# Half-height second score products in an fp32r attention and FFN kernel, and another order of a tick's stages

## The chip, the cores and the metric

The kernel runs on one NeuronCore of a Trainium2 chip. The metric is the device time of one execution in microseconds. Before the change the median of three runs is 1044.72 us (1044.53 to 1045.08). A separate execution with the hardware profiler on supplies the rows that are read below.

## The reference

```python
scores = scale * np.matmul(q, k.transpose(0, 1, 3, 2))      # 8 batches, 8 heads, 576 x 64
mask = (rel >= 0) & (rel < 128)                             # causal, window of 128
attn = softmax(np.where(mask, scores + bias, -1e9))         # bias: ALiBi slopes per head
x = np.matmul(attn, v)                                      # -> (4608, 512)
h = x @ w_in                                                # 512 -> 2048
out = (h * sigmoid(1.702 * h)) @ w_out                      # 2048 -> 512
```

All inputs are float32. A row of queries sees at most 128 keys, so a block of 128 queries needs two blocks of 128 keys.

## The kernel before

TensorE's fast format here is fp32r, which keeps fewer bits than fp32. To keep the precision, an operand x is split into a high part (x cast to fp32r) and a low part (x minus that, again in fp32r), and a product is put together from several fp32r products.

**Blocks and units.** Batch 0 is treated apart, in plain fp32 (units that the code calls whole). For batches 1 to 7, two heads of 576 rows lie side by side as one head pair of 1152 rows, cut into nine blocks of 128 queries. A unit is one or two successive blocks: for batches 2 to 7 each pair has four units of two blocks and one unit of one block. A block's scores have 256 columns (its own keys and those before), the first block of a pair 128.

**The operands of a score product.** q and k come in transposed and doubled: the 64 features stand in partitions 0 to 63 and again in 64 to 127. `split_q` (L770) casts the whole doubled q to fp32r into the tile Q; `split_rest` (L792) casts k into K1, replaces the lower half of Q (partitions 64 to 127) by q's low part, and writes k minus K1 into K2, again doubled. So in Q one half holds the high part and the other half the low part, and a product over 128 partitions adds both at once. `scores` (L819) issues two products for each block, K1 and then K2, both with Q's 128 rows, accumulated in one PSUM bank that both blocks share (`s_ps`, one buffer):

```python
for z, ks in enumerate((u.K1, u.K2)):
    nc.tensor.matmul(to, u.Q.t[:, q], ks.t[:, k], start=(z == 0), stop=(z == 1))
```

The fourth of these partial products, low times low, comes along for free.

**The other stages of a unit.** `biased` (L860, DVE) adds bias and mask and takes the row minimum; `exponents` (L879, ACT); `normal` (L890, POOL, DVE or ACT) multiplies by the reciprocal of the sum; `flip` (L912, TensorE) transposes the probabilities into a PSUM buffer `t_ps`, of which there are two (tag "t"); `high` and `low` (L938, L943) split the transposed probabilities; `load_v` and `split_v` bring in and split the values; `mix` (L953) multiplies by them, and `sum_up` (L985) adds the halves and, for later rows, stores the result to DRAM by a DMA from SP's queue.

**What sets the order.** A software pipeline works on several units at once: `tick` (L1260) issues each stage for another unit, so that a unit passes through in about five ticks. Between ticks come the FFN's steps: `up` (L1068, 12 products for one 128-wide slice of the 2048) and `down` (L1184). The loop at L1331 runs through the FFN's steps and calls as many ticks as the due times ask. Each operation goes into a plan with an estimated duration. Up to 340 us of planned time (`CUT`) the planner's greedy `order` (L325) fixes the order of every engine's queue by these estimates; the rest is issued in the plan's own order (`rest`, L425) and placed by the framework's scheduler. PSUM has eight banks: two accumulators of the FFN, two for `h_ps`, one each for `s_ps` and `x_ps`, two for `t_ps`.

**Array forms.** A matmul's operands fix which part of the array of TensorE it uses. The profile writes it as rows*columns: 128*128 for most, 64*128 for operands of 64 partitions. In batch 0, where a head's 64 features are the contraction, score products (L850) are 64*128; some of its mix products (L967) are 128*64, or 64*128 for a last chunk of 64 keys.

Of the kernel before, what the change touches and what calls it, by code (L numbers as in the profile page):

```python
# [8 lines left out]
F32 = mybir.dt.float32  # L9
# [10 lines left out]
B, H, S, D = 8, 8, 576, 64  # L20
DM, DFF = 512, 2048
NT = B * S
P = 128
HALF = P // 2
NP = H // 2
# [25 lines left out]
LAX = {"w": 1000, "hi": 800, "lo": 0, "gl": 300, "cast": 0, "xl": 600, "p": 500}  # L51
# [7 lines left out]
SAFE = 60  # L59
REST = 400  # L60
FAR = 7
PACE = 32
LATE = 14
FAST = {c: range(0, 7) if c > LATE else range(2, 7) for c in range(LATE, NCH)}
# [400 lines left out]
def tile_kernel(ctx: ExitStack, tc: tile.TileContext, q0, k0, v0, qT, kT, v, w_in, w_out, out):  # L465
    nc = tc.nc
# [9 lines left out]
    add = plan.add  # L476

    def buf(pool, shape, dtype, tag, slots=1, name=None):
        return Buf(plan, pool, shape, dtype, tag, slots, name)
# [9 lines left out]
    def act_cast(n):  # L489
        return 104 + 0.8 * n  # L490
# [10 lines left out]
    def pool_two(n):  # L501
        return 140 + 2.17 * n

    def copy_on(e, dst, src):
        (nc.scalar.copy if e == "ACT" else nc.vector.tensor_copy)(dst, src)  # L505

    def less_on(e, dst, a, b):
        (nc.gpsimd if e == "POOL" else nc.vector).tensor_tensor(dst, a, b, ALU.subtract)  # L508
# [13 lines left out]
    def less_ways(n):  # L522
        return {"DVE": (dve_one(n), True)}
# [246 lines left out]
    def split_q(u):  # L770
        if u.whole:
            return
        u.Q = buf(att, [P, 2 * P], F32R, "Q", 2)
        add("ACT", lambda e: copy_on(e, u.Q.t[:, :u.nq], u.rq.t[:, :u.nq]), act_cast(u.nq), r=[u.rq], w=[u.Q],
            chain="split_q", ways=cast_ways(u.nq), behind=gates[32 * 2 - 1 - 32])

    def split_v(u):
# [10 lines left out]
        for i, c in enumerate(u.loaded):  # L788
            c.vbuf = u.VV
            c.v = lambda i=i, c=c: u.VV.t[:c.n, i].rearrange("p a d -> p (a d)")  # L790

    def split_rest(u):  # L792
        if u.whole:
            return
        u.K1 = buf(att, [P, 3 * P], F32R, "K1", 2)
        u.K2 = buf(att, [P, 3 * P], F32R, "K2", 2)
        add("ACT", lambda e: copy_on(e, u.K1.t[:, :u.nk], u.rk.t[:, :u.nk]), act_cast(u.nk),
            r=[u.rk], w=[u.K1], chain="K1", ways=cast_ways(u.nk), auto="DVE")
        add("POOL", lambda e: less_on(
            e, u.Q.t[D:, :u.nq], u.rq.t[D:, :u.nq], u.Q.t[D:, :u.nq].bitcast(F32)), pool_two(u.nq),  # L800
            r=[u.rq], w=[u.Q], port=True, chain="Q", ways=less_ways(u.nq), lax=LAX["lo"])
        add("POOL", lambda e: less_on(
            e, u.K2.t[:, :u.nk], u.rk.t[:, :u.nk], u.K1.t[:, :u.nk].bitcast(F32)), pool_two(u.nk),
            r=[u.rk, u.K1], w=[u.K2], port=True, chain="K2", ways=less_ways(u.nk), lax=LAX["lo"])
# [13 lines left out]

    def scores(u):  # L819
        if early(u):  # L820
            u.s = buf(ps, [P, 2, 2 * P], F32, "h", 2, name="s_h")
        else:
            u.s = buf(ps, [P, 2, 2 * P], F32, "s", 1, name="s_ps")
        ns = 0
        runs, reads = [], []
        for e, b in enumerate(u.blocks):
            n = b.end - b.first
            if u.whole:
                lo = b.q0 - u.at
                qr, q = columns(0, u, lo, b.rows)  # L830
                at, k = b.first, lo - P + b.first
                while at < b.end:
                    m = min(b.end - at, T - k % T)
                    kr, ks = columns(1, u, k, m)
                    runs.append((e, b, at, m, q, ks))
                    reads += [r for r in (qr, kr) if r not in reads]
                    ns += max(1.72 * m, 220)
                    at, k = at + m, k + m
            else:
                ko = b.q0 - P + b.first - u.k0  # L840
                qs = slice(b.q0 - u.q0, b.q0 - u.q0 + b.rows)
                ks = slice(ko, ko + n)
                ns += 2 * max(0.465 * n, 86)
                runs.append((e, b, b.first, n, qs, ks))

        def run():
            for e, b, at, n, q, k in runs:
                to = u.s.t[:b.rows, e, at:at + n]
                if u.whole:
                    nc.tensor.matmul(to, q(), k(), start=True, stop=True)  # L850
                else:
                    for z, ks in enumerate((u.K1, u.K2)):
                        nc.tensor.matmul(to, u.Q.t[:, q], ks.t[:, k], start=(z == 0), stop=(z == 1))  # L853

        u.scored = add("PE", run, ns, 165, r=reads if u.whole else [u.Q, u.K1, u.K2], w=[u.s],
            chain="scores", kind="S" if u.whole else "R")
        if early(u):
            u.scored.beside = units[u.n - 1].scored

    def biased(u):  # L860
        u.mins = small(u, 0, "mins")
        for e, b in enumerate(u.blocks):
            if first(u):
                b.p = Part(works[u.n // 2], (u.n % 2, e), lambda t, i=u.n % 2 * 2 + e: t[:, i])
            else:
                b.p = buf(att, [P, 2 * P], F32, "pb", 5)
            for head, ra, rb, cs in b.heads:
                if cs > b.live:
                    add("POOL", lambda b=b, ra=ra, rb=rb, cs=cs: nc.gpsimd.memset(b.p.t[ra:rb, b.live:cs], MOST),
                        230, w=[b.p.key_at()])  # L870
                on = ra if u.joined else 0
                add("DVE", lambda b=b, e=e, head=head, ra=ra, rb=rb, cs=cs, on=on: nc.vector.tensor_tensor_reduce(  # L872
                    b.p.t[ra:rb, cs:b.end], u.s.t[ra:rb, e, cs:b.end], bias[ra:rb, head, on + cs:on + b.end],
                    -SCALE, BIG, ALU.add, ALU.min, u.mins.t[ra:rb, e:e + 1]),
                    75 + 1.05 * (b.end - cs), 150, r=[u.s], w=[b.p.key_at(), u.mins.key_at(e)], chain="biased")
            if b.live > b.first:
                add("POOL", lambda b=b: nc.gpsimd.memset(b.p.t[:, :b.live], 0.0), 120, w=[b.p.key_at("z")])

# [376 lines left out]
            due.append((len(units), b * S // T, start) if b < 4 else (len(units), PACE * (b - 3), 5))  # L1255
    units += [None] * 4
    loads = [u for u in units if u and not u.whole]
    ticks = 0

    def tick():  # L1260

        nonlocal ticks
        n = ticks

        def stage(k, *steps):
            u = units[n + k] if 0 <= n + k < len(units) else None
            for step in steps:
                if u:
                    step(u)

        stage(1, split_q)
        stage(-2, flip, split_v)
        stage(0, load_v)
        stage(-1, biased)
        stage(1, split_rest)
        stage(-1, exponents)
        stage(-1, normal)
        stage(-2, high)
        stage(-2, low)
        stage(0, scores)  # L1280
        stage(-3, mix)
        if n + 1 < len(units) and units[n + 1] and not units[n + 1].whole and loads:
            load(loads.pop(0))
        ticks += 1
# [46 lines left out]
    for now, (j, f) in enumerate(flat):  # L1331

        if halves < 2 * NF:
            owed += max(
                (2 * g + 2 - halves - owed) / max(need[g] - DECODE_AHEAD - now, 1)
                for g in range(halves // 2, NF))
            while owed >= 1 and halves < 2 * NF:
                owed -= 1
                g, ws = halves // 2, (w1, w2)[halves % 2]
                fetch_upto(g + 1 + FETCH_AHEAD)  # L1340
                ws[g] = decode(ws[g], f"w{1 + halves % 2}_{g}", gates[2 * GATE - 1])
                halves += 1

        pace, last = 0.0, 0
        for n, by, start in due:
            if start > seen:
                break
            last = n + 3
            end = starts[by] if start != 5 else starts[6] + by
            pace = max(pace, (n + 3 - ticks - credit) / max(end - 1 - SLACK - now, 1))  # L1350
        credit += pace
        while credit >= 1 and ticks < last:
            credit -= 1
            tick()
        if j.c in FOLDS:
            if f == 2:
                folding = fold(FOLDS[j.c])
            if f > 1:
                next(folding, None)
        if f == 6 and FAR <= j.c + 1 < NCH:  # L1360
            fetch_x(j.c + 1)
        if j.c == LATE and f % 2 == 0 and f // 2 < 7:
            unfold((f // 2 + 2) % 7)
        if now + 1 < len(flat):
            nj, nf = flat[now + 1]
            if nj is j:
                j.up(nf)
            else:
                begin(nj)
                seen = max(seen, nj.c)  # L1370
        j.down(f)
        if f == j.f1 - 1:
            j.finish()

# [80 lines left out]
```

## Time and profile before

| | |
|---|---|
| median of three runs | 1044.72 us |
| the profiled execution | 1044.83 us, its span 1043.0 us |
| granted TensorE clock | 0.999 |
| TensorE busy | 1029.4 us, 99% of the span |
| weight loads | 937.7 us |
| DVE, ACT, POOL busy | 793.5, 655.8, 530.6 us |
| score products of batches 1 to 7 (L853) | 504 |
| they start between | 82.4 and 841.9 us |

Rows of a timeline give the start, the duration, engine, line, operation, the tile written and those read, the form of the array, the shape of the moving operand, and how many successive instructions were put together. Successive matmuls overlap, so a duration is the way of one through the array, while the interval from start to start is what it takes of TensorE's time. PEld is the load of the stationary operand, which can run under the matmul before it. Lines are those of the kernel before.

### The profile page before, as it was taken

What the parts mean: (1) busy time and instruction counts of PE and PEld (TensorE: products, weight loads), DVE (VectorE), ACT (ScalarE), POOL (GpSimd) and SP (SyncE); (2) the same over time, 40 slices, a digit from 0 to 9 for tenths busy, and PEclk for the clock granted to TensorE, in tenths of its full rate; (3) what the DMA queues carried; (4) which work ended last, traced back from release to release, by engine and by line L of the source; (5) the groups of instructions that cost most, each with busy time, mean ns of one, the idle gap of its engine ahead of it and who ended that gap; (6) DMA issues with size and microseconds to landing.
All of it is one profiled execution on the core that took longest, in us unless ns stands there. A gap on an engine that the chain in (4) does not pass through costs nothing.

```text
span 1043.0 us, 23177 instructions
## 1 busy us (share of the span) xinstructions
PE 1029.4 (99%) x7220; PEld 937.7 (90%) x7220; DVE 793.5 (76%) x2464; ACT 655.8 (63%) x1962; POOL 530.6 (51%) x804
## 2 busy tenths in 40 slices
PE   9999999999999999999999999999999999999998
PEld 5777888988888999999999999999999999999997
DVE  8999988899978888768686777768766744667574
ACT  7999877677745666666666666666666643344443
POOL 3343445344423467576666757666666623333342
PEclk9999999999999999999999999999999999999999
DMA  9734233333322333434333433424242354001000
GB/s 355 303 96 141 61 88 95 80 81 98 83 76 65 103 101 94 141 90 129 95 114 106 122 104 101 126 76 150 79 117 67 113 169 140 21 22 41 2 22 21
DMA packets 122027, 106.65 MB, mean 102 GB/s; under 512 B 48880, under 2 KB 111984, under 8 KB 121904
## 3 DMA queue, kind: packets, MB, share of 16 engines
q1 hardware_dynamic: 116720, 95.73, 31.2%
q10 hardware_dynamic: 5184, 9.44, 2.5%
q8 instruction: 57, 0.93, 0.4%
q14 instruction: 66, 0.54, 0.2%
HBM read 82.58 MB, written 22.54 MB: 101 GB/s over the span
## 4 chain that ended last, share of the span: by engine, by line
PE 88%; DVE 8%; issue 2%; ACT 2%; POOL 0%; DMA 0%; DVEq 0%; ACTq 0%; POOLq 0%
PE h_ps L1074 35%; PE acc L1197 28%; PE s_ps L853 5%; PE t_ps L928 5%; PE x_ps L973 5%; PE m L1162 3%; PE acc L1162 2%; PE s_ps L850 1%; PE x_ps L967 1%; DVE g L1091 1%; DVE wc L592 1%; DVE pb L872 1%; DVE w_ps L589 1%; PE idle L556 1%; DVE gl L508 1%
## 5 line engine op out<-in xcount | busy, mean ns | idle before, releaser
L1074 PE MATMUL h_ps<-xh,w 128*128 128x256 f32 x2304 | 358.7, 283 | 0.3
L1074 PEld LDWEIGHTS h_ps<-xh,w 128*128 128x128 f32 x2304 | 316.9, 188 | 18.4 <-DVE g L1091 1.7
L1197 PE MATMUL acc<-w,gh 128*128 128x512 f32 x928 | 259.5, 396 | 0.0
L1074 PE MATMUL h_ps<-xl,w 128*128 128x256 f32 x1152 | 187.3, 280 | 0.0
L508 POOL TENSOR_TENSOR gl<-g,gh 128x256 fp32r<-128x256 f32 x169 | 131.7, 781 | 107.5 <-ACT gh L505 68.2
L1197 PEld LDWEIGHTS acc<-w,gh 128*128 128x128 f32 x928 | 157.6, 189 | 19.3 <-issue 0.2
L1074 PEld LDWEIGHTS h_ps<-xl,w 128*128 128x128 f32 x1152 | 158.2, 188 | 2.3
L884 ACT ACTIVATE pb<-pb,mins 128x256 f32<-128x256 f32 (+2 forms) x272 | 132.3, 487 | 39.5 <-DVE mins L872 29.8
L508 POOL TENSOR_TENSOR Q<-rq,Q 64x256 fp32r<-64x256 f32 (+1 forms) x136 | 94.9, 698 | 117.9 <-issue 25.6
L1091 DVE SCALAR_TENSOR_TENSOR g<-g,h_ps 128x256 f32<-128x256 f32 x236 | 97.6, 413 | 72.5 <-ACT g L1090 70.9
L1090 ACT ACTIVATE g<-h_ps 128x256 f32<-128x256 f32 x236 | 90.1, 382 | 92.7 <-PE h_ps L1074 69.7
L1197 PE MATMUL acc<-w,gl 128*128 128x512 f32 x464 | 148.1, 397 | 0.0
L508 POOL TENSOR_TENSOR K<-rk,K 128x384 fp32r<-128x384 f32 (+1 forms) x121 | 109.7, 907 | 69.8 <-ACT Q L505 23.8
L505 ACT CAST gh<-g 128x256 fp32r<-128x256 f32 x184 | 74.6, 405 | 66.8 <-DVE g L1091 60.5
L872 DVE CUSTOM_DVE_ANT_0 pb<-s_ps,bias 128x256 f32<-128x256 f32 (+2 forms) x304 | 110.6, 377 | 5.5 <-PE s_ps L853 1.6
L853 PE MATMUL s_ps<-K,Q 128*128 128x256 f32 (+1 forms) x504 | 92.0, 298 | 2.4 <-DVE mins L872 1.4
L928 PE MATMUL t_ps<-ident,pb 128*128 128x128 f32 x516 | 91.0, 273 | 2.7 <-DVE wc L592 2.4
L505 ACT CAST ph<-t_ps 128x512 fp32r<-128x512 f32 (+2 forms) x133 | 68.8, 518 | 34.3 <-PE t_ps L928 25.7
L1197 PEld LDWEIGHTS acc<-w,gl 128*128 128x128 f32 x464 | 79.3, 188 | 11.8 <-POOL gl L508 0.5
L947 DVE TENSOR_TENSOR pl<-t_ps,ph 128x512 fp32r<-128x512 f32 (+2 forms) x140 | 84.6, 604 | 5.8 <-ACT ph L505 5.3
L907 DVE TENSOR_SCALAR pb<-pb,rec 128x256 f32<-128x256 f32 (+2 forms) x192 | 76.5, 430 | 2.5
L853 PEld LDWEIGHTS s_ps<-K,Q 128*128 128x128 f32 x504 | 69.7, 189 | 8.9 <-DVE mins L872 1.8
(184 smaller groups left out, 1748.3 us busy)
## 6 DMA issues: line engine op xcount, KB each, us to landing
rk<-kT SPq DMA_DIRECT2D x84, 192.0 KB, 2.5
rq<-qT SPq DMA_DIRECT2D x112, 128.0 KB, 2.3
out<-o ACTq DMA_DIRECT2D x34, 256.0 KB, 2.9
rw<-w_in SPq DMA_DIRECT2D x16, 512.0 KB, 8.6
rw<-w_out SPq DMA_DIRECT2D x16, 512.0 KB, 9.5
rk<-kT SPq DMA_DIRECT2D x56, 128.0 KB, 2.2
far<-wmh SPq DMA_DIRECT2D x56, 128.0 KB, 1.9
rv<-v SPq DMA_DIRECT2D x100, 64.0 KB, 2.0
```

Source lines behind the costliest of these rows:

```text
L505: (nc.scalar.copy if e == "ACT" else nc.vector.tensor_copy)(dst, src)
L508: (nc.gpsimd if e == "POOL" else nc.vector).tensor_tensor(dst, a, b, ALU.subtract)
L853: nc.tensor.matmul(to, u.Q.t[:, q], ks.t[:, k], start=(z == 0), stop=(z == 1))
L872: add("DVE", lambda b=b, e=e, head=head, ra=ra, rb=rb, cs=cs, on=on: nc.vector.tensor_tensor_reduce(b.p.t[ra:rb, cs:b.end], u.s.t[ra:rb, e ...
L884: nc.scalar.activation(live, live, AF.Exp, bias=u.mins.t[:b.rows, e:e + 1], scale=-1.0, accum_out=u.sums.t[:b.rows, e, 0:1])
L907: (nc.gpsimd if on == "POOL" else nc.vector).tensor_scalar(live, live, rec, None, ALU.mult)
L928: nc.tensor.transpose(u.t.t[:c.n, w:w + b.rows], b.p.t[:b.rows, col:col + c.n], ident[:b.rows, :b.rows])
L947: add("DVE", lambda m=m, a=a, z=z: nc.vector.tensor_tensor(u.pl.t[:m, a:z], u.t.t[:m, a:z], u.ph.t[:m, a:z].bitcast(F32), ALU.subtract), d ...
L1074: nc.tensor.matmul(h.t, w.t[:, z, k * P:(k + 1) * P], x[k].t, start=(part == 0 and k == 0), stop=(part == 2 and k == NC - 1))
L1090: add("ACT", lambda: nc.scalar.activation(g.t, h.t, AF.Tanh, scale=0.851), act_psum(T), r=[h], w=[g], shift=-NEXT)
L1091: add("DVE", lambda: nc.vector.scalar_tensor_tensor(g.t, g.t, 1.0, h.t, ALU.add, ALU.mult), dve_one(T), r=[h], w=[g], shift=-NEXT)
L1197: nc.tensor.matmul(acc.t, g.t[:, t * P:(t + 1) * P], w.t[:, z], start=new[t], stop=(f == self.f1 - 1 and n == 2), skip_group_check=bool(se ...
```

## The change

For batches 2 to 7 (`apart`, with `ROWS = 2`) the second score product of a block, with K2, uses only the high half of Q: 64 rows. For the first block of a unit these are partitions 0 to 63, for the second block 64 to 127. To have the high part there, Q's low part is written to the lower half for the first block's columns and to the upper half for the second block's, in two operations. The first products of both blocks are issued first, then the two half-height ones, which go to different halves of the array and to different PSUM banks: the second block's scores get a buffer of their own (`s_t`), taken from the two of `t_ps`. A unit of one block has one half-height product. The product low times low is dropped there.

From the tick before batch 2's first unit on (`OLD`), a tick's stages are issued in another order, and ticks are issued after `down` of an FFN step in place of before `up`.

```diff
+        for i, b in enumerate(u.blocks if apart(u) else u.blocks[:1]):
+            at, cols = slice(D, P) if i == 0 else slice(0, D), slice(b.q0 - u.q0, b.q0 - u.q0 + b.rows) if apart(u) else slice(0, u.nq)
+            n = cols.stop - cols.start
+            add("POOL", lambda e, at=at, cols=cols: less_on(
+                e, u.Q.t[at, cols], u.rq.t[at, cols], u.Q.t[at, cols].bitcast(F32)), pool_two(n),
+                r=[u.rq, (u.Q, "all")], w=[(u.Q, i)], port=True, chain="Q", ways=less_ways(n), lax=LAX["lo"])
...
         if early(u):
-            u.s = buf(ps, [P, 2, 2 * P], F32, "h", 2, name="s_h")
+            s = buf(ps, [P, 2, 2 * P], F32, "h", 2, name="s_h")
+        elif not apart(u):
+            s = buf(ps, [P, 2, 2 * P], F32, "s", 1, name="s_ps")
+        if not apart(u):
+            u.s = [Part(s, None, lambda t, e=e: t[:, e]) for e in range(len(u.blocks))]
         else:
-            u.s = buf(ps, [P, 2, 2 * P], F32, "s", 1, name="s_ps")
+            u.s = [Part(buf(ps, [P, 2 * P], F32, tag, n, name=name), None, lambda t: t)
+                for b, (tag, n, name) in zip(u.blocks, (("s", 1, "s_ps"), ("t", 2, "s_t")))]
...
-                ns += 2 * max(0.465 * n, 86)
+                ns += max(0.465 * n, 106) if apart(u) else 2 * max(0.465 * n, 86)
...
+        ns += 119 if apart(u) else 0
...
+                else:
+                    nc.tensor.matmul(to, u.Q.t[:, q], u.K1.t[:, k], start=True, stop=False)
+            if apart(u):
+                for e, b, at, n, q, k in runs:
+                    on = slice(e * D, e * D + D)
+                    nc.tensor.matmul(u.s[e].t[:b.rows, at:at + n], u.Q.t[on, q], u.K2.t[on, k], start=False, stop=True)
...
+        if n < OLD:
...
+        else:
+            stage(-2, split_v)
+            stage(1, split_q)
+            stage(-3, mix)
+            stage(-2, flip)
+            stage(-1, biased)
+            stage(-1, exponents)
+            stage(1, split_rest)
+            stage(-2, high)
+            stage(-2, low)
+            stage(0, scores)
+            stage(0, load_v)
+            stage(-1, normal)
...
-        while credit >= 1 and ticks < last:
-            credit -= 1
-            tick()
+        if ticks < OLD:
+            while credit >= 1 and ticks < last:
+                credit -= 1
+                tick()
...
         j.down(f)
+        if ticks >= OLD:
+            while credit >= 1 and ticks < last:
+                credit -= 1
+                tick()
```

More of the change, by code (lines that the diff above doesn't have):

```diff
@@ L61 @@
 FAR = 7
+ROWS = 2
 PACE = 32
@@ L773, in split_q @@
         u.Q = buf(att, [P, 2 * P], F32R, "Q", 2)
-        add("ACT", lambda e: copy_on(e, u.Q.t[:, :u.nq], u.rq.t[:, :u.nq]), act_cast(u.nq), r=[u.rq], w=[u.Q],
+        add("ACT", lambda e: copy_on(e, u.Q.t[:, :u.nq], u.rq.t[:, :u.nq]), act_cast(u.nq), r=[u.rq], w=[(u.Q, "all")],
             chain="split_q", ways=cast_ways(u.nq), behind=gates[32 * 2 - 1 - 32])
@@ L790, in split_v, with apart @@
             c.v = lambda i=i, c=c: u.VV.t[:c.n, i].rearrange("p a d -> p (a d)")
+    def apart(u):
+        return u.pair // NP >= ROWS
     def split_rest(u):
@@ L798, in split_rest @@
             r=[u.rk], w=[u.K1], chain="K1", ways=cast_ways(u.nk), auto="DVE")
-        add("POOL", lambda e: less_on(
-            e, u.Q.t[D:, :u.nq], u.rq.t[D:, :u.nq], u.Q.t[D:, :u.nq].bitcast(F32)), pool_two(u.nq),
-            r=[u.rq], w=[u.Q], port=True, chain="Q", ways=less_ways(u.nq), lax=LAX["lo"])
+        for i, b in enumerate(u.blocks if apart(u) else u.blocks[:1]):
[4 more added lines that the diff above has]
+                r=[u.rq, (u.Q, "all")], w=[(u.Q, i)], port=True, chain="Q", ways=less_ways(n), lax=LAX["lo"])
         add("POOL", lambda e: less_on(
@@ L842, in scores @@
                 ks = slice(ko, ko + n)
-                ns += 2 * max(0.465 * n, 86)
+                ns += max(0.465 * n, 106) if apart(u) else 2 * max(0.465 * n, 86)
                 runs.append((e, b, b.first, n, qs, ks))
+        ns += 119 if apart(u) else 0
         def run():
             for e, b, at, n, q, k in runs:
-                to = u.s.t[:b.rows, e, at:at + n]
+                to = u.s[e].t[:b.rows, at:at + n]
                 if u.whole:
                     nc.tensor.matmul(to, q(), k(), start=True, stop=True)
-                else:
+                elif not apart(u):
                     for z, ks in enumerate((u.K1, u.K2)):
                         nc.tensor.matmul(to, u.Q.t[:, q], ks.t[:, k], start=(z == 0), stop=(z == 1))
-        u.scored = add("PE", run, ns, 165, r=reads if u.whole else [u.Q, u.K1, u.K2], w=[u.s],
+                else:
[4 more added lines that the diff above has]
+                    nc.tensor.matmul(u.s[e].t[:b.rows, at:at + n], u.Q.t[on, q], u.K2.t[on, k], start=False, stop=True)
+        u.scored = add("PE", run, ns, 165, r=reads if u.whole else [u.Q, u.K1, u.K2], w=[x.buf for x in u.s[:2 if apart(u) else 1]],
             chain="scores", kind="S" if u.whole else "R")
@@ L872, in biased @@
                 add("DVE", lambda b=b, e=e, head=head, ra=ra, rb=rb, cs=cs, on=on: nc.vector.tensor_tensor_reduce(
-                    b.p.t[ra:rb, cs:b.end], u.s.t[ra:rb, e, cs:b.end], bias[ra:rb, head, on + cs:on + b.end],
+                    b.p.t[ra:rb, cs:b.end], u.s[e].t[ra:rb, cs:b.end], bias[ra:rb, head, on + cs:on + b.end],
                     -SCALE, BIG, ALU.add, ALU.min, u.mins.t[ra:rb, e:e + 1]),
-                    75 + 1.05 * (b.end - cs), 150, r=[u.s], w=[b.p.key_at(), u.mins.key_at(e)], chain="biased")
+                    75 + 1.05 * (b.end - cs), 150, r=[u.s[e].buf], w=[b.p.key_at(), u.mins.key_at(e)], chain="biased")
             if b.live > b.first:
@@ L1257, in tile_kernel @@
     loads = [u for u in units if u and not u.whole]
+    OLD = next(i for i, u in enumerate(units) if u.pair // NP >= 2) - 1
     ticks = 0
@@ L1269, in stage @@
                     step(u)
[L1271 to L1281, printed above, removed]
+        if n < OLD:
+            stage(1, split_q)
+            stage(-2, flip, split_v)
+            stage(0, load_v)
[9 more added lines that the diff above has]
+            stage(-2, split_v)
+            stage(1, split_q)
+            stage(-3, mix)
+            stage(-2, flip)
+            stage(-1, biased)
+            stage(-1, exponents)
+            stage(1, split_rest)
+            stage(-2, high)
+            stage(-2, low)
+            stage(0, scores)
+            stage(0, load_v)
+            stage(-1, normal)
         if n + 1 < len(units) and units[n + 1] and not units[n + 1].whole and loads:
```

## The prediction

> **What bounds the kernel now.** I read the page's totals first, then the stretches, then TensorE's waits, then single stretches of the timeline in order of start.
>
> ```profile
> span 1043.0 us, 23177 instructions
> PE 1029.4 (99%) x7220; PEld 937.7 (90%) x7220; DVE 793.5 (76%) x2464; ACT 655.8 (63%) x1962; POOL 530.6 (51%) x804
> PE 88%; DVE 8%; issue 2%; ACT 2%; POOL 0%; DMA 0%; DVEq 0%; ACTq 0%; POOLq 0%
> ...
> 150.00:340.00 190.00, 187.45 (x1293) 168.77 (x1292) 162.42 (x584) 124.47 (x370) 75.40 (x119) 1.00 0.30 81
> 340.00:600.00 260.00, 259.60 (x1805) 239.97 (x1805) 203.02 (x626) 168.00 (x536) 168.27 (x253) 1.00 0.38 109
> 600.00:842.00 242.00, 242.00 (x1672) 223.53 (x1671) 173.34 (x543) 152.22 (x486) 152.29 (x233) 1.00 0.37 105
> ...
> PE t_ps L928 <- DVE wc L592: 2.4, 6, 0.6
> PE s_ps L853 <- DVE mins L872: 1.4, 5, 0.3
> ```
>
> The third line is the chain of waits that ended last: 88% TensorE. In the stretch rows (length, then busy time of PE, PEld, DVE, ACT, POOL, then the granted clock, 1.00) TensorE is idle for 2.6, 0.4 and 0.0 us of 692. So between 150 and 842 us, where the changed units run, the end is set by the sum of TensorE's start-to-start intervals: what the change adds to or takes from that sum reaches the end in full. DVE, ACT and POOL have a sixth to a half of their time free there. The longest wait of TensorE for anything is 0.6 us.
>
> **The products that are touched.**
>
> ```profile
> L853 PE MATMUL s_ps<-K,Q 128*128 128x256 f32 x448 | 85.1, 300 | 1.7 <-DVE mins L872 1.2
> L853 PE MATMUL s_ps<-K,Q 128*128 128x128 f32 x56 | 11.5, 281 | 0.7 <-DVE xf L1033 0.4 <-DVE mins L872 0.2
> ...
> 201.86 0.38 PE L928 MATMUL t_ps<-ident,pb 128*128 128x128 f32 x2
> 202.00 0.72 PE L853 MATMUL s_ps<-K,Q 128*128 128x256 f32 x4
> 202.55 0.28 PE L973 MATMUL x_ps<-ph,VV 128*128 128x256 f32 x1
> ```
>
> 504 products are 28 head pairs x 9 blocks x 2. The change applies to batches 2 to 7, that is 24 pairs; by the unit lists each pair has four units of two blocks (the first of them with a 128-column block) and one unit of one block: 72 + 24 + 24 = 120 units. Means of 300 ns are not prices, since matmuls overlap; start-to-start intervals are. Two transposes from 201.86 at 0.11 each (below) end their turn at 202.08; four products then last until 202.55, 0.118 us each, and the neighbours of other lines join without a gap. All of these carry the form 128*128 (rows by columns of the array).
>
> **What a half-height product costs.** The changed second products have 64 rows, so their form is 64*128. The only matmuls of that form in this trace are batch 0's, and they show three things.
>
> ```profile
> 39.57 0.28 PE L1074 MATMUL h_ps<-xl,w 128*128 128x256 f32 x1
> 39.78 0.71 PE L850 MATMUL s_ps<-k,q 64*128 64x128 f32 x4
> ...
> 68.50 0.27 PE L967 MATMUL x_ps<-pw,v 128*128 128x128 f32 x1
> 68.70 0.37 PE L967 MATMUL x_ps<-pw,v 64*128 64x128 f32 x1
> 68.92 0.27 PE L967 MATMUL x_ps<-pw,v 64*128 64x128 f32 x1
> 69.12 0.38 PE L1074 MATMUL h_ps<-xh,w 128*128 128x256 f32 x1
> ...
> 500.58 0.63 PE L1074 MATMUL h_ps<-xh,w 128*128 128x256 f32 x4
> ```
>
> ```profile
> 11.34 0.27 PE L850 MATMUL s_h<-k,q 64*128 64x128 f32 x1
> ...
> 11.45 0.38 PE L850 MATMUL s_h<-k,q 64*128 64x256 f32 x1
> 11.46 0.38 PE L850 MATMUL s_ps<-k,q 64*128 64x256 f32 x1
> 11.67 0.38 PE L850 MATMUL s_h<-k,q 64*128 64x256 f32 x1
> 11.68 0.38 PE L850 MATMUL s_ps<-k,q 64*128 64x256 f32 x1
> 11.99 0.33 PE L928 MATMUL t_ps<-ident,work 128*128 128x128 f32 x1
> ...
> 11.98 0.14 PEld L928 LDWEIGHTS t_ps<-ident,work 128*128 128x128 f32 x1 [0.33 <-issue]
> ```
>
> First, two of them on different halves of the array do run beside each other: the s_h and s_ps products start 0.01 us apart (11.67 and 11.68) and cost one interval of 0.22.
>
> Second, **entering the form** costs time. In one form 256 columns take (0.63 - 0.28) / 3 = 0.117 us, so after 39.57 the next start would be 39.69; it is 39.78, 0.09 late. Four 128-column products take 3 x 0.11 + 0.27 = 0.60 (interval 11.34 to 11.45, duration 0.27) but the row has 0.71: another 0.11 within the first. Together 0.20. The step 68.50 to 68.70, same line and type, gives 0.09 + (0.37 - 0.27) = 0.19.
>
> Third, **leaving it** costs as much: from 68.92 the next start is due at 69.03 and comes at 69.12, and that product lasts 0.38 in place of 0.28: 0.19. Into a transpose, 11.68 + 0.22 = 11.90 against 11.99, and 0.33 against 0.27: 0.15. The PEld row shows why: the next weight load, which otherwise starts as its predecessor's matmul does, is held back (0.33 us idle, waiting for nothing that the profile names) until the other form's matmul is through.
>
> The Trainium skill (TensorEngine Tiling (Array Packing), Tiling Modes, Key Properties) says that changing the tiling mode, and not merely the tile, drains TensorE. The trace agrees, at 0.15 to 0.20 us for each change, and by that rule this change pays twice for each unit; without it the result is the first rival below.
>
> So a round trip costs 0.34 (exit into a transpose) to 0.39 us (exit into a product whose weights are fp32r, as those of the FFN and of the mix are). I take 0.39: the scores of 202.00 are followed by the mix, and in the new order scores stand last among TensorE's steps of a tick, ahead of FFN products. That both ends of such a change could be fp32r isn't in the trace: batch 0's half-height products are fp32 and their neighbours of either kind. The lower bound for that is the late start alone, 0.09 + 0.09 = 0.18.
>
> **The sum.** The first products (K1) stay: two intervals of 0.118.
> - 72 units of two 256-column blocks: removed 2 x 0.118 = 0.236; added 0.39 + 0.118 + 0.013 for the pair = 0.521. Net +0.285, in all +20.5 us.
> - 24 units with a 128-column first block: its second product is worth 0.06 (half) to 0.118; I take 0.11, the transposes' interval. Net 0.521 - 0.228 = +0.293, in all +7.0 us.
> - 24 units of one block: nothing lies beside the half-height product, so it saves nothing and pays the round trip: +0.39, in all +9.4 us.
>
> That is +36.9 us. By 0.34 and the dearer 128-column product it is 16.9 + 5.6 + 8.2 = +30.7; by the cheaper one and 0.39, +38.1; by 0.18, 5.4 + 2.0 + 4.3 = +11.7.
>
> **Edits I cost at nothing.**
>
> ```profile
> L508 POOL TENSOR_TENSOR Q<-rq,Q 64x256 fp32r<-64x256 f32 x108 | 79.8, 739 | 88.5 <-issue 24.2 <-ACT K L505 17.5 <-ACT ph L505 7.6
> L508 POOL TENSOR_TENSOR Q<-rq,Q 64x128 fp32r<-64x128 f32 x28 | 15.2, 541 | 29.4 <-DVE wsum L636 18.8 <-ACT K L505 5.5 <-DVE mins L872 1.6
> rv<-v SPq DMA_DIRECT2D x100, 64.0 KB, 2.0
> ```
>
> Q's low half becomes two operations in 96 units: 2 x 541 - 739 = 343 ns each, 33 us more for POOL (or DVE), which is free for some 300 of those 692 us. If uncovered, K2's low half behind it and so the scores are 0.34 us later per unit. Bias steps wait for one bank each in place of the shared one, a small relief.
>
> The reordered steps add no instruction. The value load (load_v) now goes to SP's queue behind the mix's stores of sums, whose issue waits for DVE; its data are wanted two ticks later, and a tick is about 692 / 120, 5.8 us, so a landing of 2.0 us is covered by the FFN's products; uncovered, ACT's cast of V and POOL's V split behind it would be some 2 us late, three ticks ahead of the mix. The normal step goes last and is wanted by the next tick's transposes; what hides it is the FFN step between. On ACT, Q's cast and the mix's xb copy now stand ahead of the exponents, and the tick as a whole stands behind the FFN's down step: up's tanh and g come first on ACT and DVE. TensorE waits for none of them for over 0.6 us now, and with 35 us more on TensorE every other engine gains slack. From reordering I see at most the 3.0 us of idle PE to win in these stretches, and as a loss 0.6 us in one unit of ten, 7 us. I take a gain of 2, half of it drain time that falls into such waits.
>
> **Total:** 1044.83 us is the profiled execution (span 1043.0 and 1.8 around it); the median of the runs is 1044.72, so 0.1 less. 1044.7 + 36.9 - 2 = 1079.6, say **1079.5 us**. The forecast's own range is 1068 to 1092.
>
> **Rivals.**
>
> *No drain between fp32r forms: faster.* Then the pair costs 0.131 in place of 0.236 (or 0.228): 72 x 0.105 + 24 x 0.097 = 9.9 us saved, 1034.8 us. For it: the 0.01 us of 11.67 and 11.68, and that no change between two fp32r forms is in the trace. Against: 39.57 to 39.78 leaves an fp32r product and 68.92 to 69.12 enters one, and both pay. It decides below 9.9 / 120 = 0.083 us per round trip, under a quarter of what I read. Chance 0.14. The Trainium skill (TensorE: Matmul & The Clock Gate, Part 3, The mechanism) puts a packed group at one matmul plus about 4 ns per tile; taken alone that is this rival, and it says nothing of the way in and out.
>
> *A cheaper drain,* 0.18 per round trip by the late starts alone: +11.7, 1054 to 1068. Chance 0.08. Near break-even, within 0.2%: 0.04.
>
> *The halves don't run beside each other:* the change then doesn't do what it says, and the second half adds its interval, 96 x 0.105 = 10 us more, 1090 us. Against it is the same pair of rows. Chance 0.04.
>
> *The transposes' banks become the wait.* The second block's scores take one of the two banks of t_ps.
>
> ```profile
> 499.77 0.27 PE L928 MATMUL t_ps<-ident,pb 128*128 128x128 f32 x1
> 501.67 0.68 DVE L947 TENSOR_TENSOR pl<-t_ps,ph 128x512 fp32r<-128x512 f32 x1
> 501.33 0.41 DVE L872 CUSTOM_DVE_ANT_0 pb<-s_ps,bias 128x256 f32<-128x256 f32 x1
> ```
>
> If each unit waited for one bias step (0.41 us), 120 x 0.41 = 49 us came on top, 1129 us. Against: transposes hold a bank for 502.35 - 499.77 = 2.6 us, and a tick gives two banks 11.6 us. Chance 0.02.
>
> **Chances and range.** 0.68 for the forecast, and the rivals 0.14, 0.08, 0.04, 0.04, 0.02. Slower by over 0.2% (2.1 us, about what a measurement of this kernel can tell from no change): 0.68 + 0.08 + 0.04 + 0.02 = 0.82; within it 0.04; faster 0.14. The range 1054 to 1092 holds forecast, cheap drain and serial halves, 0.80.
>
> **What would show it.** Right: rows of 64*128 products with starts 0.01 apart, the first some 0.2 us late and 0.1 us longer than its partners of today, the next 128*128 product likewise; PE busy near 99% still, with 35 us more of it before 842's counterpart, spread evenly over the units. Wrong: the weight load of the half-height product starting under its predecessor as 128*128 loads do (then 1035), TensorE waiting for bias steps at t_ps (then over 1092), or starts of the two halves 0.12 apart (1090).

## The result, and the profile after

The changed kernel takes 1095.05 us (median of six runs, 1094.68 to 1099.36) against 1044.62 us for the kernel before (six runs): a ratio of 1.0489, 95% interval 1.0473 to 1.0505, slower. The profiled execution took 1094.84 us, its span is 1093.1 us, so the span grew by 50.1 us. The forecast had the sign and the engine right. It added up 36.9 us for the changes of form, less 2 for the new order; 50.1 came, and 1095.05 lies 3 us above its range (1068 to 1092).

The page of the changed kernel: span, totals, the chain that ended last, and the granted clock in forty slices.

```profile
span 1093.1 us, 23225 instructions
PE 1081.3 (99%) x7220; PEld 950.2 (87%) x7220; DVE 806.0 (74%) x2463; ACT 663.5 (61%) x1960; POOL 550.5 (50%) x903
...
PEclk9999999999999999999999999999999999999999
...
PE 73%; DVE 4%; issue 1%; ACT 0%; DVEq 0%; ACTq 0%
```

The same 7220 matmuls, at the same clock, keep TensorE busy for 1081.3 us in place of 1029.4. It is still the bound. POOL was busy for 20 us more, DVE for 13 and ACT for 8, and all three stay far from full.

Its stretches (length, then busy time and count of PE, PEld, DVE, ACT, POOL) and TensorE's longest waits:

```profile
150.00:340.00 190.00, 189.59 (x1265) 166.86 (x1264) 157.67 (x565) 121.93 (x360) 83.19 (x145) 1.00 0.29 81
340.00:600.00 260.00, 259.75 (x1650) 225.11 (x1649) 190.05 (x580) 157.17 (x488) 154.91 (x260) 1.00 0.34 97
600.00:842.00 242.00, 241.67 (x1530) 209.52 (x1529) 169.40 (x501) 143.82 (x449) 148.20 (x249) 1.00 0.34 97
...
PE t_ps L948 <- DVE wc L593: 1.8, 5, 0.5
PE idle L557 <- POOL ident masks.py:199: 1.4, 1, 1.4
```

The counts show where the time went. From 150 to 340 us TensorE got through 28 matmuls fewer than before (1265 against 1293), from 340 to 842 us through 297 fewer (3180 against 3477). Nearly all of the loss lies behind 340 us, where the planner's order ends and the framework's scheduler places the work. The two waits shown are from the first 150 us. From there to 340 us the profile names one wait of TensorE, of 0.2 us, and behind 340 us none at all (shorter ones than 0.15 us it doesn't list).

What TensorE does instead is in the timeline of the changed kernel. L869 is a first product, L873 a half-height one.

```profile
607.05 0.28 PE L869 MATMUL s_t<-K,Q 128*128 128x256 f32 x1
607.26 0.38 PE L873 MATMUL s_ps<-K,Q 64*128 64x256 f32 x1
607.26 0.38 PE L873 MATMUL s_t<-K,Q 64*128 64x256 f32 x1
607.57 0.38 PE L993 MATMUL x_ps<-ph,VV 128*128 128x256 f32 x1
```

This is the unit as the prediction drew it. After 607.05 the next start is due at 607.17 and comes at 607.26 (0.09 late); both halves start in the same hundredth and last 0.38 in place of 0.28 (0.10 late); the mix product is due 0.118 + 0.10 behind 607.26, at 607.48, comes at 607.57 (0.09) and lasts 0.38 (0.10). From 607.17 to 607.67 the pair takes 0.50 us: a round trip of 0.38 and one interval.

Seven microseconds earlier stands the other kind.

```profile
600.72 0.28 PE L869 MATMUL s_t<-K,Q 128*128 128x256 f32 x1
600.93 0.38 PE L873 MATMUL s_ps<-K,Q 64*128 64x256 f32 x1
601.24 0.39 PE L993 MATMUL x_ps<-ph,VV 128*128 128x256 f32 x1
601.47 0.28 PE L993 MATMUL x_ps<-pl,VV 128*128 128x256 f32 x1
601.59 0.28 PE L993 MATMUL x_ps<-ph,VV 128*128 128x256 f32 x1
601.79 0.38 PE L873 MATMUL s_t<-K,Q 64*128 64x256 f32 x1
602.10 0.38 PE L993 MATMUL x_ps<-pl,VV 128*128 128x256 f32 x1
```

The two halves of one unit are torn apart by three mix products of another. The array goes into the half-height form and out of it twice, and nothing lies beside either half: two groups of half-height products (a group is what stands in that form without another product between), of 0.51 us each. The PEld rows show the loads of 600.93 and 601.24 held back until 0.07 us before the recorded end of the other form's product (601.00 and 601.31). The load of 600.50, ahead of the change, starts 0.22 us before its matmul:

```profile
600.50 0.19 PEld L869 LDWEIGHTS s_t<-K,Q 128*128 128x128 f32 x1
600.93 0.18 PEld L873 LDWEIGHTS s_ps<-K,Q 64*128 64x128 f32 x1 [0.25 <-issue]
601.24 0.19 PEld L993 LDWEIGHTS x_ps<-ph,VV 128*128 128x128 f32 x1
```

Counted over all starts, there are 163 groups of half-height products, not 120: 24 of one-block units, 53 pairs together, and 43 pairs torn into two. All 43 lie behind 340 us; the 24 pairs before it are whole.

Tearing itself isn't new. In the trace of before, behind 340 us, 5 of 71 two-block units have their four products torn apart, as here by two transposes:

```profile
369.05 0.51 PE L853 MATMUL s_ps<-K,Q 128*128 128x128 f32 x3
369.39 0.39 PE L928 MATMUL t_ps<-ident,pb 128*128 128x128 f32 x2
369.53 0.36 PE L853 MATMUL s_ps<-K,Q 128*128 128x256 f32 x1
```

There all products have one form, so tearing cost nothing: the two transposes and the product behind them take 0.34 us, 369.39 to 369.73, no more than 2 x 0.11 + 0.118.

**From start to start.** What the groups cost in all can be added up from the starts in the traces. In the trace of before, a product of 256 columns takes 0.1175 us of TensorE's time, one of 512 columns 0.232, a transpose or a 128-column score product 0.11 (medians from start to start); call this its turn. The cost of a group is the time from the start of the product ahead of it to the start of the second product behind it, less the turns of the full-height ones among them; a wait in that stretch counts as the group's. All other time beyond the turns, from 150 us to the end, is called late starts here; it hangs a little on the turns taken, and only its differences between kernels are read. In the changed kernel the 163 groups cost 81.2 us: the median is 0.51 for a pair of 256-column halves and for a single one, 0.56 for a pair with a 128-column half, 0.40 for a 128-column half alone. The removed products' turns were 25.2, so the change of form costs 56.0 us. Late starts fall from 11.2 us before to 5.7, and 56.0 - 5.5 = 50.5, against 50.1 of span.

### The profile page after: what moved, and what is told of

Read it like the earlier page. It is cut to its first block, busy times and chain, and to the rows that moved or that the text cites. A ratio compares the mean times of both kernels' runs of the same rounds, so it can differ in the third digit from the quotient of the medians.

```text
span 1093.1 us, 23225 instructions
## 1 busy us (share of the span) xinstructions
PE 1081.3 (99%) x7220; PEld 950.2 (87%) x7220; DVE 806.0 (74%) x2463; ACT 663.5 (61%) x1960; POOL 550.5 (50%) x903
## 4 chain that ended last, share of the span: by engine, by line
PE 73%; DVE 4%; issue 1%; ACT 0%; DVEq 0%; ACTq 0%
PE h_ps L1094 30%; PE acc L1217 22%; PE x_ps L993 5%; PE t_ps L948 4%; PE s_ps L873 3%; PE m L1182 3%; PE acc L1182 2%; DVE xl L509 2%; PE s_t L873 1%; PE s_t L869 1%; PE s_ps L869 1%; DVE o L1200 1%; DVE xh L506 1%; DVE g L1111 0%; DVE K L506 0%
## 5 line engine op out<-in xcount | busy, mean ns | idle before, releaser
L1094 PE MATMUL h_ps<-xh,w 128*128 128x256 f32 x2304 | 368.9, 286 | 0.1
L509 POOL TENSOR_TENSOR gl<-g,gh 128x256 fp32r<-128x256 f32 x166 | 126.9, 764 | 148.5 <-ACT gh L506 105.3
L1094 PE MATMUL h_ps<-xl,w 128*128 128x256 f32 x1152 | 193.0, 282 | 0.7
L509 POOL TENSOR_TENSOR Q<-rq,Q 64x128 fp32r<-64x128 f32 (+1 forms) x227 | 112.2, 494 | 84.2 <-issue 25.1
L509 POOL TENSOR_TENSOR K<-rk,K 128x384 fp32r<-128x384 f32 (+1 forms) x127 | 114.5, 901 | 35.9 <-PE s_t L873 18.4
L509 POOL TENSOR_TENSOR VV<-rv,VV 128x128 fp32r<-128x128 f32 (+2 forms) x123 | 57.7, 470 | 71.0 <-ACT VV L506 43.3
L948 PE MATMUL t_ps<-ident,pb 128*128 128x128 f32 x516 | 88.4, 276 | 2.7 <-DVE wc L593 1.8
L892 DVE CUSTOM_DVE_ANT_0 pb<-s_ps,bias 128x256 f32<-128x256 f32 (+5 forms) x208 | 76.3, 368 | 13.6 <-PE s_ps L873 8.9
L1131 POOL TENSOR_TENSOR gl<-g,gh 128x128 fp32r<-128x128 f32 (+1 forms) x52 | 31.6, 608 | 81.6 <-ACT gh L1128 63.7
```

What stands on the lines that cost most here:

```text
L948: nc.tensor.transpose(u.t.t[:c.n, w:w + b.rows], b.p.t[:b.rows, col:col + c.n], ident[:b.rows, :b.rows])
L1094: nc.tensor.matmul(h.t, w.t[:, z, k * P:(k + 1) * P], x[k].t, start=(part == 0 and k == 0), stop=(part == 2 and k == NC - 1))
```

## The experiments

The theory: each group of half-height products costs a way into the form and out of it, and the loss follows the number of groups. The rivals: the second bank taken from the transposes, Q's low part in two operations, or the ticks' order make waits. Kernels measured together share their runs of the kernel before, whose median was 1044.4 to 1044.6.

### Parts undone

**Full height again.** Everything stays as changed, but the second products use all 128 rows.

```diff
-                    on = slice(e * D, e * D + D)
+                    on = slice(0, P)
```

> The changed kernel with one thing undone: the second products use all 128 rows of Q again (form 128*128). Banks, Q's split in two operations, issue order K1 K1 K2 K2 and the ticks' order stay as changed. Theory (changes of form cost it): no 64*128 product is left after 95 us, so the whole loss goes: 1037 to 1046 us, below 1044.6 as far as the new order wins something. Rival (the shared banks or the ticks' order make the waits): the loss stays for the greater part, over 1060 us.

Measured: 1053.79 us, ratio 1.0088 (1.0071 to 1.0105). Of the 50 us of loss, 41 go with the form alone. But 9 us stay, which the theory did not expect. The waits of TensorE in this run:

```profile
PE h_ps L1094 <- DVE xl L509: 4.4, 7, 0.7
PE t_ps L948 <- DVE wc L593: 1.9, 5, 0.4
...
PE h_ps L1094 <- DVE g L1111: 0.8, 3, 0.3
```

The FFN's first products wait for the split of x on DVE, seven times, once in about every 58 us. One of the seven:

```profile
587.30 0.28 PE L1094 MATMUL h_ps<-xl,w 128*128 128x256 f32 x1
588.21 0.39 PE L1094 MATMUL h_ps<-xl,w 128*128 128x256 f32 x1 [0.63 <-DVE xl L509]
588.43 0.28 PE L1094 MATMUL h_ps<-xh,w 128*128 128x256 f32 x1
```

The profile counts 0.63 us as idle, but the wait costs 588.43 - 587.30 - 2 x 0.1175 = 0.89: idle time begins only when the recorded 0.28 of the product before are over, and the product behind the wait holds TensorE for 0.10 longer. Seven of them are 6.2 us of the 9. All late starts of this run come to 20.1 us, 8.9 more than before. In the changed kernel the wait isn't there, and late starts are 5.7. The two kernels' matmuls stand in the same order on TensorE, at 7218 of 7220 places, so the difference between them is the form's and not the layout's: 56.0 us of cost, less the 14.4 us of late starts that go with it, are 41.6 where 41 were measured.

**The ticks' order alone.** `ROWS = 9`, so no unit has its products apart.

> Products, Q and banks as before the change; the ticks' new order alone. Theory: TensorE's sum of intervals is that of before, 1037 to 1046 us; if the accounts of the changed kernel (163 round trips at 0.39 less what the pairs save is 58 us, 50 were measured) are right, the order wins up to 8 us. Rival (the order costs it): over 1060 us.

Measured: 1045.80 us, ratio 1.0012 (1.0002 to 1.0021). The order neither wins the 8 us nor costs the loss.

**The half-height products alone,** in the order and place of ticks before the change (`OLD = len(units)`).

> The half-height products in their two banks, with the ticks' order and place as before the change. 156 groups: 60 pairs, 96 single ones (36 torn pairs and 24 one-block units). By the prices read in the changed kernel's trace, a pair together +0.27 us, a torn one +0.74, a one-block unit +0.385: 16 + 27 + 9 = 52, less the 5 us of waits that such drains took over there, 1092 us (1087 to 1096). Rival (the ticks' order makes the loss): under 1070 us.

Measured: 1097.27 us, ratio 1.0506 (1.0485 to 1.0527), 1 us above the theory's range and far from the rival's. The ticks' order isn't needed for the loss. Nor is it alone what tears pairs: with the order of before, 36 of the 72 pairs behind 340 us are torn here; with the new order and the products of before (the run above), the four products are torn in 33 of 70 units, where tearing changes no form.

### The number of groups changed

**Pairs kept together.** Past the planned stretch, each half-height product may be issued only behind the one before it, the first of them behind both first products.

```diff
+                    for ins in nc.cur_bb.bb.instructions[n0:] if free else ():
+                        tc.add_manual_dep(ins, prev.name, mybir.DependencyInfo(
+                            mybir.DependencyClass.NoSync, mybir.DependencyReason.DATA))
```

> The changed kernel, but past the planned 340 us the half-height products of a unit may be issued only behind both first products, one after the other; 36 of the 43 torn pairs come together, and there are 127 groups of half-height products in place of 163. Theory (each group costs a round trip of 0.39 us and each torn pair 0.105 more): 36 x 0.495 = 18 us less than the changed kernel's 1095, 1077 us (1073 to 1082). Rival (the loss is in waits for banks or in POOL's extra work): the products wait longer for one another, 1090 to 1105 us.

Measured: 1078.82 us, ratio 1.0327 (1.0312 to 1.0343). 36 groups fewer are worth 16.2 us, 0.45 each.

**Two round trips for each unit.** The half-height product right behind the first product of its block, K1 K2 K1 K2.

```diff
                     nc.tensor.matmul(to, u.Q.t[:, q], u.K1.t[:, k], start=True, stop=False)
-            if apart(u):
-                for e, b, at, n, q, k in runs:
-                    on = slice(e * D, e * D + D)
-                    nc.tensor.matmul(u.s[e].t[:b.rows, at:at + n], u.Q.t[on, q], u.K2.t[on, k], start=False, stop=True)
+                    on = slice(e * D, e * D + D)
+                    nc.tensor.matmul(to, u.Q.t[on, q], u.K2.t[on, k], start=False, stop=True)
```

> The changed kernel, but each block's half-height product comes right behind its first product: K1 K2 K1 K2. No pair is side by side and there are 216 groups of half-height products in place of 163. Theory: 53 more groups at 0.39 + 0.105 is 26 us more than 1095, 1121 us (1116 to 1127). Rival (the number of changes of form doesn't matter): 1095 plus the 53 x 0.105 = 6 us of the lost pairs, 1101 us.

Measured: 1117.91 us, ratio 1.0702 (1.0680 to 1.0723). 53 groups more cost 22.9 us, 0.43 each; the measured time lies inside the theory's range. A group of that run in its timeline:

```profile
599.97 0.36 PE L869 MATMUL s_ps<-K,Q 128*128 128x256 f32 x1
600.26 0.38 PE L871 MATMUL s_ps<-K,Q 64*128 64x256 f32 x1
600.57 0.39 PE L1092 MATMUL h_ps<-xh,w 128*128 128x256 f32 x1
```

600.26 to 600.57 is 0.31 for a product of 0.118, and the FFN's product behind it lasts 0.39 in place of 0.28.

**Pairs together, one-block units at full height.** As the run with pairs kept together, and `apart` also asks for two blocks.

> As the run with pairs kept together, and units of one block keep their full-height second product: 103 groups of half-height products, of them 89 pairs. Theory (a change into the form and out of it is paid by each group): a one-block group cost 0.626 us where the full-height pair of products cost 0.240, so 24 x 0.385 = 9.2 us less than 1078.8, 1069.6 us (1067 to 1072). Rival (one-block units aren't slower, since their drain hides waits): 1077 to 1080 us.

Measured: 1070.07 us, ratio 1.0245 (1.0228 to 1.0262). 24 groups fewer are worth 8.75 us, 0.365 each; expected were 0.385. A one-block unit pays for a change of form that saves it nothing.

Tearing costs about the same in both directions, 0.43 to 0.45 us for each group more. The last two columns are the sums from start to start:

| half-height products | groups | of them pairs | us | cost of the groups | late starts |
|---|---|---|---|---|---|
| none, the kernel before | 0 | 0 | 1044.6 | 0 | 11.2 |
| none, ticks' order alone | 0 | 0 | 1045.80 | 0 | 12.9 |
| pairs together, one-block units full | 103 | 89 | 1070.07 | 53.5 | 6.2 |
| pairs together | 127 | 89 | 1078.82 | 65.3 | 5.5 |
| ticks' order of before | 156 | 60 | 1097.27 | 79.5 | 9.0 |
| the changed kernel | 163 | 53 | 1095.05 | 81.2 | 5.7 |
| two round trips | 216 | 0 | 1117.91 | 107.7 | 1.9 |

The row of the ticks' order of before doesn't follow the number of groups: 7 groups fewer than the changed kernel, and 2.2 us slower. Its groups are cheaper by 1.7, its late starts dearer by 3.3. In every row the cost of the groups, less the removed turns (22.4 us with one-block units at full height, 25.2 in the others), plus the change of the late starts gives the measured difference to the kernel before within 1 us.

### What is left of the full-height run

**One operation for Q's low part,** at full height, with two banks and the order K1 K1 K2 K2.

> As the run with full-height second products, but Q's low part is again one operation, for the lower half alone; two banks for a unit's scores, the order K1 K1 K2 K2 and the ticks' new order stay. It parts what made that run 8 us slower than the ticks' order alone (1045.8). If it is the split in two operations (POOL and DVE busier, the FFN's h_ps waiting for xl on DVE): 1045 to 1048 us. If it is the banks: 1052 to 1055 us.

Measured: 1049.99 us, ratio 1.0054 (1.0039 to 1.0069). Neither figure: half of the 8 us is gone.

**Two operations for Q's low part** with the score products and the bank of before, in the ticks' new order.

> Score products and bank as before the change, the ticks' new order, and Q's low part of batches 2 to 7 in two operations, each for one block's columns: for the second block low and high part change places in Q, which alters no sum over all 128 rows. If the split in two makes the 8 us of the run with full-height products: 1050 to 1054 us. If it doesn't: 1045 to 1048 us.

Measured: 1042.90 us, ratio 0.9985 (0.9974 to 0.9996). That is below both figures: the two operations cost nothing here, and it is the only kernel under the one before.

**The same with the ticks' old order.**

> As the run with Q's low part in two operations, the ticks' order as before the change. That run came out at 1042.9, 1.7 us under the kernel before. If the two operations win it: 1041 to 1043.5 us. If it is the scheduler's luck with one order of the work: 1044 to 1048 us.

Measured: 1050.32 us, ratio 1.0048 (1.0033 to 1.0064), outside both figures. So the 1042.9 isn't won by the two operations. These five kernels without any half-height product past batch 0 lie between 1042.9 and 1053.8 us, with the same matmuls in other layouts. Their late starts go from 9.3 to 20.1 us, 10.8 of the 10.9 us between them. In the full-height run, 6.2 us are the seven waits for xl, which the run with one operation doesn't have; why DVE splits x late there, these runs don't say. An effect of a few us can't be put down to one edit here.

### No torn pairs, by the plan

**The planner's order to the end** (`CUT = 2000000`), for the kernel before as the control and for the changed one, whose four products are one step of the plan.

> The kernel before, with the planner's order to the end in place of up to 340 us. It is the control for the next run; from 1040 to 1060 us, since the planner's prices are estimates.

> The changed kernel with the planner's order to the end: a unit's four products are one step of the plan, so no pair is torn, 120 groups of half-height products as the prediction counted. Theory (0.27 us for a unit of two 256-column blocks, 0.29 with a 128-column one, 0.385 for a one-block unit): 19.4 + 6.9 + 9.2 = 36 us over the control, 31 if waits are taken over as in the changed kernel. Rival (torn pairs weren't the reason for the part that the prediction missed): 45 to 55 us over the control.

Measured: 1070.47 us for the control, above what was expected of it, and 1092.13 us for the changed one. The difference is 21.7 us, below what the theory gave (31 to 36) and far below the rival. The control is itself 26 us slower than the kernel before: its late starts are 36.9 us, against 11.2. The longest waits that the profile names in both; the first row is of the control, the second and third of the changed one:

```profile
PE s_ps L853 <- DVE mins L872: 7.0, 13, 0.8
```

```profile
PE x_ps L993 <- DVE xs L1034: 5.8, 15, 0.4
...
PE s_ps L864 <- DVE mins L892: 0.3, 1, 0.3
```

The scores' wait for the bias step, 7.0 us, is gone in the changed one, which has a wait of the mix in its place. From start to start, the 120 groups cost 62.9 us, 37.7 more than the removed turns, and late starts are 22.5 in place of 36.9: 37.7 - 14.4 = 23.3, against 23.5 of span. So the price of 120 groups is close to the 36.9 us that the prediction gave them, and the two kernels' times differ by less since the control had late starts to lose.

## Why the prediction was right and where it failed

**What bounds the kernel:** right. The loss is time of TensorE at the same clock, and waits for other engines didn't grow: late starts fell.

**The price of half-height products:** right, and right for fp32r on both sides, which the trace of before could not show. Predicted were 0.39 us for a round trip and 0.131 for a pair side by side, 0.521 together; the unit at 607 has 0.50, and the median of such pairs is 0.51. For a single half-height product 0.39 + 0.118 = 0.508 was said, and 0.51 is the median. The halves do start together, and the weight loads are held back as they were in batch 0. The rivals "no drain", "a cheaper drain" and "the halves don't run beside each other" are out. So is "the transposes' banks": no row of a wait for them is among TensorE's. The Trainium skill (TensorEngine Tiling (Array Packing), Tiling Modes, Key Properties) says that changing the tiling mode drains TensorE. The trace agrees, at about 0.19 us for each way.

**The count failed.** The prediction wrote "72 + 24 + 24 = 120 units" and charged each one round trip. It took for granted that a unit's four products run in a row, as in its rows at 202 us, which lie in the planned stretch. Behind 340 us the framework's scheduler places single instructions; the 5 torn units of before, such as the one at 369.05, could have been seen, but not that there would be 43. Of the 72 pairs there, 43 were torn, each costing a second round trip and the half that no longer lies beside anything. So the extra time isn't spread evenly over the units, as the prediction's signs of being right had it. By the prediction's own prices 163 groups are 163 x 0.39 + 110 x 0.118 + 53 x 0.131 = 83.5, less the removed 192 x 0.118 + 24 x 0.11 = 25.3: 58.2 us in place of 36.9. From start to start it is 56.0, and for 120 groups, in the run planned to the end, 37.7: the prices hold and the count was wrong. The run with pairs together shows that tearing is a cause and not a sign: 36 groups fewer, 16.2 us less.

**What it then overstates.** 58.2 against 50.1 us of span. Of these 8 us, 2.2 are price (mostly that a torn 128-column half costs 0.40 in place of 0.508), and 5.5 are late starts that went. The prediction saw "at most the 3.0 us of idle PE to win" and took 1 us of waits that a drain fills. That bound was misread: idle time leaves out every late start that hides under the recorded length of the matmul before, and the trace of before has 11.2 us of late starts. The slope of 0.45 us in the run with pairs together, against the expected 0.39 + 0.105 = 0.495, is price too: there late starts hardly moved (5.7 and 5.5). In the run with two round trips they fell by 3.8.

**Reordering:** a gain of 2 was taken, half of it for the order itself; the order alone measured 1.2 us slower (0.2 to 2.2). The prediction's bounds, 3 to win and 7 to lose, hold it.

The two errors, the count and the late starts, have opposite signs, and the forecast missed its range by only 3 us because of that.

## What to carry to other kernels

Count how often the array changes its form, not only how many matmul rows a packing saves: here a round trip costs 0.38 us, over three intervals of a 256-column product, and a pair of half-height products saves one. An estimate from these numbers: four pairs in a row would pay for one round trip. No run here had more than one pair in a group. A unit that has only one such product pays and saves nothing. And count in the order that is issued, not in the order that is written: what a scheduler may place one by one, it may tear.

A kernel at 99% busy may still have late starts to lose. They show in the starts, not in the idle time.

## What the runs showed of the hardware

That the halves run side by side was plain from batch 0; here the second starts 3 to 4 ns behind the first in all 53 pairs. That leaving the form is as dear as entering it, also between two fp32r matmuls, was the open point: the product behind a half-height one starts 0.09 us late and lasts 0.38 to 0.39 us in place of 0.28, whether it is of the mix (601.24, 607.57) or of the FFN (600.57 in the run with two round trips).

Unexpected was how the same matmuls without any change of form spread: 1042.9 to 1053.8 us over five layouts. Behind 150 us, no single idle time of TensorE in the slowest of them is over 0.7 us. One such wait, 0.63 us by the profile, took 0.89 of TensorE's time.
